# Sliding-window attention with a gated mixture: another order of the steps, one TensorE tiling, masks on other engines

## The chip, the cores and the metric

The kernel runs on one core of one Trainium2 chip. The metric is the device time of one execution in microseconds (us), the median of several runs. A core has five engines that run their own instruction queues side by side: TensorE (PE in the profile, with its weight loads as PEld), VectorE (DVE), ScalarE (ACT), GpSimd (POOL) and SyncE (SP, which here only issues transfers). An instruction that waits holds up everything behind it in its own engine's queue.

## The reference

```python
x = A_x                                    # [1, 2048, 512], bfloat16
g = sigmoid((x * gate_w).sum(-1))          # one gate per token
# A: attention, 32 heads of 16, query i sees keys i-255 .. i
qkv = x @ wqkv
scores = q @ k.T * 16 ** -0.5;  scores = where(mask, scores, -1e9)
a = softmax(scores) @ v @ wo
# B: the 8 tokens with the largest r = x @ w_r get a feed-forward, the others stay
y = (silu(x_sel @ w_gate) * (x_sel @ w_up)) @ w_down * sigmoid(r_sel)
b = x.at[idx].add(y)
out = g * a + (1 - g) * b                  # [1, 2048, 512]
```

## The kernel before

**Units of work.** The 512 channels are four chunks `c` of 8 heads, the 2048 tokens four blocks of 512. A *step* `s` is one chunk and one key block `qb`: there are sixteen, in the order `c = s // 4, qb = s % 4`, all of one chunk first. For its 16 groups of 32 keys a step computes the scores against the up to 288 queries that may see them (L717). Four heads share one matmul: `Kst` holds the keys four times, each copy masked to one head's 16 channels (L596, four DVE instructions per step). A step's scores form one stream of 4608 columns (3456 in the last block), cut into *units* of 512 columns, 136 in all. A unit has two halves of 64 channel rows, in PSUM banks 0 and 1 or 2 and 3 by turns; ACT takes the exponential of both (L731, 1024 columns) into `P`, which has two buffers, one for even and one for odd steps.

**Masks.** Where a group's window begins and ends, DVE takes the minimum of `P` and a pattern of 0 and 3e38 (L752), for every two units, with 64 columns a place.

**PV.** `pv_step` (matmuls at L771) accumulates one query block in two PSUM banks: first the eight last groups of the key block before (from the other `P` buffer), then the sixteen of its own. `Vbd` holds V by heads with columns of ones, so that the sums of the exponentials come out as extra rows. Then DVE copies the two banks to `OXY` (L801), four transfers collect the sums in `Dc`, DVE takes the reciprocal (L813), two transfers spread it over partitions as `Rb` (L814, L815), two more move the second half of `OXY`, and POOL multiplies into `OT` (L816). Steps 14 and 15 do the same by PE transposes in `norm_t` (L824 to L849).

**The rest.** `pair` runs two products side by side with 64x128 tiles of PE: keys and queries of a block (L582, copied out at L592 and L587), V (L606, copied at L613 and sent through memory to `Vbd`), and the output tiles (L663). The last four output tiles are `out_single` (L650, L656). `z_item` computes gate and router, `ffn` the feed-forward of the selected tokens, whose result is scattered into a copy of x in memory; `resid` loads that copy into `xr`, scales it by 1 - g (L633), and `out_evac` adds it to the gated output (L637) and stores it. A flag (L1021 to L1028) says whether all sums were in range; a general path (not taken) follows it.

**What sets the order.** Every operation is added to `Sched` with the tiles it reads and writes, an estimated duration and a priority. `schedule` lays them out in estimated time and so fixes each engine's queue; the chip then follows those queues, with semaphores. On PE the rule `pick_pe` takes score units first; other work goes by `prio` and a due unit `dl`, and PV is collected into bursts (`burst`), because a change of tiling is charged with `SWITCH = 106.0` ns. Banks 4 to 7 are handed out one by one (`acq`, `rel`); PV takes two and a `pair` takes two. `work` lists when each projection is due, in units: `U0(c, tc)` is the first unit of a step.

Of the kernel before, what the change touches and what calls it, by code (L numbers as in the profile page):

```python
# [49 lines left out]
class Sched:  # L50
# [6 lines left out]
    def __init__(self, nc, es, n_dma=40, banks=(4, 5, 6, 7), burst=2000):  # L57
        self.nc = nc
        self.ops = []
        self.last_w = {}  # L60
        self.readers = {}
        self.tick_sem = {e: es.enter_context(nc.semaphore("fk_" + e)) for e in self.ENGS}
        self.dsem = [es.enter_context(nc.semaphore("fd_%d" % i)) for i in range(n_dma)]
        self.nhw = n_dma
        self.dsem += [es.enter_context(nc.semaphore("fw_%d" % i)) for i in range(4)]
        self.free_banks = {b: [] for b in banks}
        self.burst = burst
        self.hold = 0.0
# [35 lines left out]
    def schedule(self):  # L104
# [13 lines left out]
        act_end = [0.0]  # L118
# [20 lines left out]
        def bank_ready(op):  # L139
            if not op.acq:  # L140
                return 0.0
            if len(self.free_banks) < len(op.acq):
                return None
            ts = sorted(max([u.t1 + self.SEM if u.done else 1e12 for u in us] or [0.0]) for us in self.free_banks.values())
            if ts[len(op.acq) - 1] >= 1e12:
                return None
            return ts[len(op.acq) - 1]
# [11 lines left out]
        def pick_pe():  # L159
            t = tfree["pe"]  # L160
            c = []
            hold = self.hold and any(o.kind == "V" and o.acq and o is vq[min(vp[0], len(vq) - 1)] and rdy(o) <= t + self.hold for o in cand["pe"])
            for o in cand["pe"]:
                if hold and o.acq and o.kind != "V" and o.prio >= 50:
                    continue
                b = bank_ready(o)
                if b is None:
                    continue
                c.append((max(rdy(o), b), o))
            if not c:  # L170
                return None
            S = [(s, o) for s, o in c if o.kind == "S"]
            V = [(s, o) for s, o in c if o.kind == "V"]
            F = [(s, o) for s, o in c if o.kind not in ("S", "V")]
            starve = act_end[0]
            s_ready = S and S[0][0] <= t + 30.0
            v = min(V, key=lambda z: z[1].id) if V else None
            if v is not None and v[0] > t + 40.0:
                v = None
            back = self.backlog(t)  # L180
            if v is not None and self.pe_mode == "V":
                room = starve - t
                if not s_ready and S == [] or room > 226 + 106 + 180 + v[1].dur:
                    return v[1], t
            if s_ready:
                return S[0][1], max(t, S[0][0])
            f = [(o.prio, o.id, o) for s, o in F if s <= t + 30.0]
            un = self.unow[0]
            urg = [z for z in f if z[2].dl is not None and un >= z[2].dl]
            if urg and self.pe_mode != "V":  # L190
                return min(urg, key=lambda z: z[:2])[2], t
            if v is not None and back >= self.burst:
                return v[1], t
            if f:
                return min(f, key=lambda z: z[:2])[2], t
            if v is not None and (back >= self.burst * 0.6 or not S):
                return v[1], t
            allc = [(s, o) for s, o in c if o.kind != "V"] or c
            s, o = min(allc, key=lambda z: (z[0], z[1].id))
            if v is not None and s > t + 400:  # L200
                return v[1], t
            if o.kind != "V" and V:
                sv, ov = min(V, key=lambda z: z[0])
                if sv + 300 < s and ov is min(V, key=lambda z: z[1].id)[1]:
                    return ov, max(t, sv)
            return o, max(t, s)

        self.unow = [0]
        vq = [o for o in ops if o.kind == "V"]
        vp = [0]  # L210

        def backlog(t):
            n = 0
            for o in vq[vp[0]:vp[0] + 60]:
                if o.done:
                    continue
                if o.acq and n:
                    break
                ok = True
                for d, sem in o.deps.items():  # L220
                    if d.kind == "V":
                        continue
                    if not d.done or (d.t1 + d.lat + (100.0 if d.dma else self.SEM)) > t + 40:
                        ok = False
                        break
                if not ok:
                    break
                n += o.cols
            return n
        self.backlog = backlog  # L230

        left = len(ops)
        while left:
# [10 lines left out]
            if e == "pe":  # L244
                if op.acq:
                    fb = sorted(self.free_banks, key=lambda b: (max([u.t1 if u.done else 1e12 for u in self.free_banks[b]] or [0.0]), b))
                    for bk in op.acq:
                        b = fb.pop(0)
                        us = self.free_banks.pop(b)
                        bk.i = b  # L250
                        for u in us:
                            op.deps[u] = True
                            start = max(start, u.t1 + self.SEM)
# [11 lines left out]
            for bk in op.rel:  # L265
                self.free_banks[bk.i] = [u for u in bk.users if u.eng != "pe"]
                dirty.add("pe")
            if not left or op.name is None and op.dur == 430:
                dirty.add("pe")
            if op.kind == "S":  # L270
                self.unow[0] += 1
            if e == "act" and op.kind == "E":
                act_end[0] = op.t1
                dirty.add("pe")
            while vp[0] < len(vq) and vq[vp[0]].done:
                vp[0] += 1
            for s in op.succ:
# [4 lines left out]
                if s.kind == "V":  # L282
                    dirty.add("pe")
# [99 lines left out]
NKB = 16  # L383
PADW = 32
STREAM = 16 * 288
PLEN = STREAM + 2 * PADW
# [4 lines left out]
def fast_path(nc, sem_es, flag, A_x, A_wqkv, A_wo, B_x, B_w_r, B_w_gate, B_w_up, B_w_down, gate_w, out):  # L391
# [4 lines left out]
    rs = nc.dram_tensor("fs_r", [16, 4096], F32, kind="Internal").ap()  # L396

    with ExitStack() as es:
# [9 lines left out]
        QT = sb("QT", [128, 2, 2048])  # L408
        Kr = sb("Kr", [128, 2, 512])
# [4 lines left out]
        Vbd = sb("Vbd", [128, 2, 64, 144])  # L414
        P = sb("P", [128, 2, 2, PLEN])
# [7 lines left out]
        kf = sb("kf", [128, 1], F32)  # L423
        xi = sb("xi", [128, 32], F32)
        NOX = 3
        OXY = sb("OXY", [128, NOX, 2, 512], F32)
        Dc = sb("Dc", [128, 2, 32], F32)
# [5 lines left out]
        xr = sb("xr", [128, 2, 4, 512])  # L433
        zb = xr[:, 0, 0, :]
# [18 lines left out]
        xsel = sb("xsel", [64, 512])  # L453
        xselT = sb("xselT", [128, 4, 32])
        WF1 = sb("WF1", [128, 4 * 1792])
        EG = sb("EG", [128, 1024], F32)
# [4 lines left out]
        ok1 = EG[:, 0:512]  # L461
        HT = xr[:, 1, 0, :].rearrange("p (b t) -> p b t", b=4)
        yq = zbf[0:8, :]
        WG = WF1[:].rearrange("p (k f) -> p k f", k=4)
# [8 lines left out]
        S.add("dve", lambda e: e.memset(zb, 0.0), w=[("xr", 0)], dur=150, prio=0)  # L473
# [12 lines left out]
        S.add("dve", lambda e: e.tensor_copy(out=kf[:], in_=hmi[:, 1:2]), r=["hmi2"], w=["kf"], prio=2)  # L486
        for i, (o_, w_) in enumerate(((ALU.is_lt, "MKb"), (ALU.is_ge, "MKa"))):
            S.add("dve", lambda e, i=i, o_=o_: e.tensor_scalar(out=MK[:, 32 * i:32 * i + 32], in0=xi[:], scalar1=kf[:, 0:1], scalar2=3.0e38, op0=o_, op1=ALU.mult),
                  r=["xi", "kf"], w=[w_], prio=2)
        MKR = ["MKa", "MKb"]  # L490
        for g in range(2):
            S.add("pool", lambda e, g=g: e.memset(P[:, g, :, 0:PADW], 0.0), w=[("padl", g)], prio=4)
            S.add("pool", lambda e, g=g: e.memset(P[:, g, :, PADW + STREAM:], 0.0), w=[("padr", g)], prio=4)

# [8 lines left out]
        S.add("pool", lambda e: e.memset(xsel[:], 0.0), w=["xsel"], dur=500, prio=20)  # L503
# [34 lines left out]
        for b in list(range(8)) + [4, 5, 6, 7, 4, 5]:  # L538
            S.add("pe", lambda e, b=b: e.matmul(ps[:, b, :], zb[:, 0:128], zb, start=True, stop=True), r=[("xr", 0)], w=[("warm", b)] + ([("S", b // 2)] if b < 4 else []), dur=430, prio=0,  # L539
                  mode="A", kind="F")  # L540
        for b in range(4, 8):
            S.free_banks[b].append(S.last_w[("warm", b)])


        def pair(A, B, prio, natom=4, dur=222.0, after=(), chain=None, gate=None, dl=None):

            bA, bB = Bank(), Bank()
            last = None
            for ph in range(2):
                for k in range(natom):  # L550
                    lo, hi = ((A, bA), (B, bB)) if ph == 0 else ((B, bB), (A, bA))
# [1372 lines left out]
```

## Time and profile before

| | |
|---|---|
| time, median of 3 runs | 198.92 us (197.67 to 199.78) |
| the profiled execution | 199.66 us, its span 196.9 us |
| granted PE clock, mean | 0.965 of full speed |
| busy, of the span | PE 164.1 us, DVE 142.8, ACT 127.3, POOL 26.8 |
| first exponential of the scores begins | 15.05 us after the span's start |
| last exponential ends | 162.6 us |
| last output addition ends | 190.6 us |

The span runs from the first to the last instruction of the program; the execution's time has some microseconds more. Busy time of PE counts overlapping matmuls once, from the first start to the last modelled end, so a PE that is 90% busy may still be fed with gaps. The times of single instructions in the profile are from this one execution.

### The profile page before, as it was taken

What the parts mean: (1) busy time and instruction counts of PE and PEld (TensorE: products, weight loads), DVE (VectorE), ACT (ScalarE), POOL (GpSimd) and SP (SyncE); (2) the same over time, 40 slices, a digit from 0 to 9 for tenths busy, and PEclk for the clock granted to TensorE, in tenths of its full rate; (3) what the DMA queues carried; (4) which work ended last, traced back from release to release, by engine and by line L of the source; (5) the groups of instructions that cost most, each with busy time, mean ns of one, the idle gap of its engine ahead of it and who ended that gap; (6) DMA issues with size and microseconds to landing.
All of it is one profiled execution on the core that took longest, in us unless ns stands there. A gap on an engine that the chain in (4) does not pass through costs nothing. (4 is left out here: it accounts for less than half of the span.)

```text
span 196.9 us, 6699 instructions
## 1 busy us (share of the span) xinstructions
PE 164.1 (83%) x2889; PEld 82.5 (42%) x2890; DVE 142.8 (72%) x365; ACT 127.3 (65%) x142; POOL 26.8 (14%) x42
## 2 busy tenths in 40 slices
PE   7889999997897998997992999778879973999910
PEld 2435555443353544553541545435345441534300
DVE  7569998997699949857534699687596454698870
ACT  3009999998599999283197598986999990000000
POOL 8400000010200202002212020032020204110000
PEclk9999999999999999999999699999999998799975
DMA  7998899993963943694678977742211232215840
GB/s 145 251 230 184 213 234 229 284 291 83 326 258 90 366 124 87 181 236 135 213 175 165 271 162 224 161 72 74 63 29 27 77 83 72 70 53 169 261 157 12
DMA packets 53058, 32.17 MB, mean 163 GB/s; under 512 B 37736, under 2 KB 49276, under 8 KB 52992
## 3 DMA queue, kind: packets, MB, share of 16 engines
q1 hardware_dynamic: 51376, 31.16, 60.1%
q10 hardware_dynamic: 1584, 0.52, 1.3%
q8 instruction: 23, 0.38, 0.9%
q14 instruction: 11, 0.09, 0.2%
q0 software_dynamic: 64, 0.02, 0.0%
HBM read 20.20 MB, written 9.42 MB: 150 GB/s over the span
## 5 line engine op out<-in xcount | busy, mean ns | idle before, releaser
L731 ACT ACTIVATE f_P<-f_ps 128x1024 bf16<-128x1024 f32 (+1 forms) x136 | 125.3, 1081 | 33.1 <-PE f_ps L771 16.7
L717 PE MATMUL f_ps<-f_QT,f_Kst 64*128 64x288 bf16 (+5 forms) x744 | 53.4, 244 | 9.6 <-ACT f_P L731 8.9
L752 DVE TENSOR_TENSOR f_P<-f_P,f_MK 128x512 bf16<-128x512 bf16 (+4 forms) x102 | 34.4, 355 | 24.4 <-ACT f_P L731 23.7
L771 PE MATMUL f_ps<-f_P,f_Vbd 64*34 64x288 bf16 (+8 forms) x1408 | 46.9, 251 | 4.6 <-DVE f_OXY L801 3.0
L717 PEld LDWEIGHTS f_ps<-f_QT,f_Kst 64*128 64x128 bf16 x744 | 21.4, 94 | 40.9 <-ACT f_P L731 33.3
L582 PE MATMUL f_ps<-f_XT,f_W 64*128 64x512 bf16 x256 | 37.0, 376 | 1.2 <-DVE f_QT L587 0.9
L771 PEld LDWEIGHTS f_ps<-f_P,f_Vbd 64*34 64x34 bf16 x1408 | 25.7, 94 | 26.2 <-issue 17.7
L816 POOL TENSOR_TENSOR f_OT<-f_OXY,f_Rb 128x512 bf16<-128x512 f32 x14 | 18.1, 1299 | 105.3 <-DMA f_Rb<-fs_r 105.3
L606 PE MATMUL f_ps<-f_W,f_XT 64*128 64x256 bf16 x256 | 17.8, 269 | 1.4 <-DMA f_XT<-in_A_x_dram 0.7
L596 DVE TENSOR_SCALAR f_Kst<-f_Kr,f_hm 128x512 bf16<-128x512 bf16 x64 | 18.6, 345 | 0.0
L801 DVE COPY f_OXY<-f_ps 128x512 f32<-128x512 f32 x28 | 18.2, 675 | 0.0
L663 PE MATMUL f_ps<-f_wo,f_OT 64*128 64x512 bf16 x96 | 13.5, 399 | 3.2 <-POOL f_OT L816 3.0
L582 PEld LDWEIGHTS f_ps<-f_XT,f_W 64*128 64x128 bf16 x256 | 10.9, 94 | 7.5 <-PE f_ps L582 1.9
L613 DVE CAST f_Vn<-f_ps 128x512 bf16<-128x512 f32 x16 | 10.5, 685 | 4.7 <-PE f_ps L606 4.7
L606 PEld LDWEIGHTS f_ps<-f_W,f_XT 64*128 64x128 bf16 x256 | 11.5, 94 | 5.5 <-DVE f_QT L587 1.4
L592 DVE CAST f_Kr<-f_ps 128x512 bf16<-128x512 f32 x16 | 10.7, 671 | 3.6 <-PE f_ps L582 3.6
L1032 ACT COPY f_sg<-f_ones_f 1x1 f32<-1x1 f32 x1 | 0.2, 190 | 17.5 <-DVE flag L1028 17.5
L813 DVE RECIPROCAL f_RC<-f_Dc 128x32 f32<-128x32 f32 x14 | 4.8, 345 | 9.2 <-DMA f_Dc<-f_OXY 9.2
L637 DVE SCALAR_TENSOR_TENSOR f_outt<-f_ps,f_g_f,f_xr 128x512 bf16<-128x512 f32 x16 | 11.3, 745 | 0.2
L587 DVE CAST f_QT<-f_ps 128x512 bf16<-128x512 f32 x16 | 10.9, 680 | 0.0
L663 PEld LDWEIGHTS f_ps<-f_wo,f_OT 64*128 64x128 bf16 x96 | 4.2, 97 | 9.0 <-POOL f_OT L816 3.1
L539 PE MATMUL f_ps<-f_xr 128*128 128x512 bf16 x14 | 5.5, 564 | 1.2 <-DVE f_hmi L476 1.2
(87 smaller groups left out, 76.2 us busy)
## 6 DMA issues: line engine op xcount, KB each, us to landing
fs_v<-f_Vn SPq DMA_DIRECT2D x8, 608.0 KB
f_Vbd<-fs_v SPq DMA_DIRECT2D x32, 144.0 KB, 3.2
f_Rb<-fs_r SPq DMA_DIRECT2D x14, 256.0 KB
f_xr<-fs_xc SPq DMA_DIRECT2D x4, 512.0 KB, 4.3
out_dram<-f_outt SPq DMA_DIRECT2D x16, 128.0 KB, 1.7
f_WF<-in_B_w_gate_dram SPq DMA_DIRECT2D x1, 1792.0 KB
f_OXY<-f_OXY SPq DMA_DIRECT2D x28, 64.0 KB, 4.3
f_WF<-in_B_w_up_dram SPq DMA_DIRECT2D x1, 1792.0 KB
```

What stands on the lines that cost most here:

```text
L582: return e.matmul(ps[:, bk.i, :], W[R, k, f0:f0 + 128], XT[R, k, 512 * tc:512 * tc + 512], start=first, stop=last, tile_position=(64 * h, ...
L587: S.add("dve", lambda e: e.tensor_copy(out=QT[:, c % 2, 512 * tc:512 * tc + 512], in_=ps[:, bk.i, :]), r=[("bk", id(bk))], w=[("QT", c % 2 ...
L596: S.add(eng, lambda e, j=j: e.tensor_scalar(out=Kst[:, s, :, j, :], in0=Kr[:, n % 2, :].rearrange("p (a k) -> p a k", k=32), scalar1=hm[:, ...
L606: return e.matmul(ps[:, bk.i, 256 * i:256 * i + 256], XT[R, kc, 128 * a:128 * a + 128], W[R, kc, 1024 + 256 * cp:1024 + 256 * cp + 256], s ...
L637: S.add("dve", lambda e: e.scalar_tensor_tensor(out=outt[:, a % 4, :], in0=ps[:, bk.i, :], scalar=g_f[:, a:a + 1], in1=xr[:, (a // 4) % 2, ...
L663: return e.matmul(ps[:, bk.i, :], OT[R, k, 128 * a:128 * a + 128], wo[R, k, :], start=first, stop=last, tile_position=(64 * h, 0), skip_gr ...
L717: ins = e.matmul(ps[:, sbk + v, so:so + m], Kst[R, ks, t, :, :].rearrange("p j k -> p (j k)"), QT[R, c % 2, q0:q0 + m], start=True, stop=T ...
L731: S.add("act", lambda e, p0=p0, n=n, sbk=sbk: e.activation(out=P[:, g, :, p0:p0 + n], in_=ps[:, sbk:sbk + 2, 0:n], func=ACT.Exp, scale=0.2 ...
L752: S.add("dve", lambda e, v=v, m=m: e.tensor_tensor(out=v, in0=v, in1=m, op=ALU.min), r=rd, w=[("M", g, r_[3]) for r_ in b], dur=60 + 2 * k ...
L771: ins = e.matmul(ps[64 * v:64 * v + 34, bk.i, q0:q0 + n], Vbd[R, cp, kh, 36 * q:36 * q + 34], P[R, g, v, PADW + o:PADW + o + n], start=fir ...
L801: S.add("dve", lambda e, b=b, bk=bk: e.tensor_copy(out=OXY[:, x, b, :], in_=ps[:, bk.i, :]), r=[("O", id(bX))], w=[("OXY", x, b, p) for p ...
L816: S.add("pool", lambda e: e.tensor_tensor(out=OT[:, c, 512 * qb:512 * qb + 512], in0=OXY[:, x, 0, :], in1=Rb[:, y, :], op=ALU.mult), r=[(" ...
```

## The change

**Order of steps.** A step is now `c = 2 * (s // 8) + s % 2, qb = s % 8 // 2`: chunks 0 and 1 block by block, then chunks 2 and 3. All queries stay in one tile `QK`; `P` has three buffers (a step reads the one before the last), `Vbd` four blocks, `OXY` four buffers. **PE.** Scores, projections, V and output all use 64x64 tiles, as PV does, so each of their matmuls becomes two; the rule for bursts goes, and PV is work with a due unit like the rest. PSUM banks 4 to 7 are handed out as two pairs, and one DVE instruction copies a pair. **Masks.** In steps 0 to 13 POOL multiplies `P` by 0 or 1 after the exponential; in steps 14 and 15 PE adds -3e38 to the scores. **Sums.** Two steps share one reciprocal; in most steps the sums go through memory (`ds`). **Space.** The feed-forward's weights and intermediate tiles lie in `xr` and `outt`; `xr` holds all four blocks.

```diff
-    def __init__(self, nc, es, n_dma=40, banks=(4, 5, 6, 7), burst=2000):
+    def __init__(self, nc, es, n_dma=40, banks=(2, 3)):
...
+            now = [z for z in c if z[0] <= t + 25.0]
+            if not now:
+                m = min(z[0] for z in c)
+                now = [z for z in c if z[0] <= m + 25.0]
+            s, o = min(now, key=lambda z: (z[1].kind != "S", z[1].dl if z[1].dl is not None else z[1].prio, z[1].id))
+            return o, s
...
+        NP = 3
+        P = sb("P", [128, NP, 2, STREAM])
...
+        WF1 = xr[:].rearrange("p q i f -> p (q i f)")[:, 0:4 * 1792]
+        EG = outt[:].rearrange("p a f -> p (a f)").bitcast(F32)
...
-                return e.matmul(ps[:, bk.i, :], W[R, k, f0:f0 + 128], XT[R, k, 512 * tc:512 * tc + 512], start=first, stop=last,
-                                tile_position=(64 * h, 0), skip_group_check=True)
+                return e.matmul(ps[64 * u:64 * u + 64, b, :], W[R, k, f0 + 64 * u:f0 + 64 * u + 64], XT[R, k, 512 * tc:512 * tc + 512], start=first, stop=last,
+                                tile_position=(64 * h, 64 * u), skip_group_check=True)
...
+        def cq(s):
+            return 2 * (s // 8) + s % 2, s % 8 // 2
+        U0 = [68 * (s // 8) + 9 * (s % 8) - (2 if s % 8 == 7 else 0) for s in range(NS)]
         TS = (14, 15)
+        DIRECT = (4, 5, 6)
+        POOLM = range(14)
...
+                    for x, (so, mc, m) in enumerate(mks):
+                        for v in range(2):
+                            R = slice(64 * v, 64 * v + 64)
+                            for w in range(2):
+                                C = slice(64 * w, 64 * w + 64)
+                                ins = e.matmul(ps[C, sbk + v, so:so + m], IDm[R, :], MB[R, mc:mc + m],
+                                               start=False, stop=(x == len(mks) - 1), tile_position=(64 * v, 64 * w), skip_group_check=True)
...
-                        S.add("dve", lambda e, v=v, m=m: e.tensor_tensor(out=v, in0=v, in1=m, op=ALU.min), r=rd, w=[("M", g, r_[3]) for r_ in b],
-                              dur=60 + 2 * k * w_ * 0.67, prio=1)
+                        S.add("pool", lambda e, v=v, m=m: e.tensor_tensor(out=v, in0=v, in1=m, op=ALU.mult), r=[("P", g, x) for x in us] + ["MK0", "MK1"],
+                              w=[("M", g) + x for r_ in bt for x in r_[3]], dur=130 + 2 * k * w_ * 2.3, prio=1)
...
+            op.dl = U0[s] + (LV if s < 8 else LW) + (tl[t][0] // 512 if s == s_src else 0)
...
-            for b, bk in enumerate((bX, bY)):
-                S.add("dve", lambda e, b=b, bk=bk: e.tensor_copy(out=OXY[:, x, b, :], in_=ps[:, bk.i, :]), r=[("O", id(bX))],
-                      w=[("OXY", x, b, p) for p in ("d", "o", "m")], dur=690, prio=4, use=(bk,), rel=(bk,))
+            S.add("dve", lambda e: e.tensor_copy(out=OXY[:, x], in_=ps[:, bk.i:bk.i + 2, :]), r=[("O", id(bk))],
+                  w=[("OXY", x, 0), ("OXY", x, 1), ("OXYm", x, 0), ("OXYm", x, 1)], dur=1220, prio=4, use=(bk,), rel=(bk,))
...
+            S.add("dve", lambda e: e.reciprocal(out=RC[:, s0:s + 1, :], in_=Dc[:, y]), r=Dk, w=[("RC", s0), ("RC", s)], dur=640, prio=3)
...
+        kq[0:2] = [(4, (0, 0, 1), (1, 1, 0)), (8, (0, 1, 0), (0, 1, 1))]
+        for dl, a, b in kq:
+            work.append((dl, 0, "kq", a, b))
         for cp in range(2):
             for tc in range(4):
-                work.append((U0(2 * cp, tc) - 8 if (cp, tc) != (0, 0) else -1, 1, "v", cp, tc))
+                work.append((U0[sidx(2 * cp, tc)] - VD if (cp, tc) != (0, 0) else 1, 1, "v", cp, tc))
         work.append((20, 2, "z"))
-        work.append((75, 2, "f"))
+        work.append((60, 2, "f"))
```

In a pair `(which, c, tc)` of `kq`, `which` is 1 for keys and 0 for queries: the second pair projects query block 1 of chunk 0 with the keys of chunk 1's first block.

## The prediction

> **What bounds it now.** I read the page's forty slices first, then the table by stage, then the waits, and last the timeline where an engine is dense.
>
> ```profile
> PE   7889999997897998997992999778879973999910
> ACT  3009999998599999283197598986999990000000
> POOL 8400000010200202002212020032020204110000
> L731 ACT ACTIVATE f_P<-f_ps 128x1024 bf16<-128x1024 f32 (+1 forms) x136 | 125.3, 1081 | 33.1 <-PE f_ps L771 16.7
> ACT f_P L731 <- PE f_ps L771: 16.7, 5, 7.2
> 80.00:90.00 10.00, 9.87 (x198) 5.28 (x194) 5.62 (x18) 5.73 (x7) 0.82 (x1) 1.00 0.81 204
> 170.00:180.00 10.00, 9.48 (x74) 3.79 (x73) 9.67 (x39) 0.00 (x0) 1.26 (x1) 1.00 0.23 70
> ```
>
> (The last two lines are the table by stage: window, length, then busy time of PE, PE's weight loads, DVE, ACT, POOL, then granted clock, DMA share, GB/s.) There are three stages. **Start:** the first exponential begins at 15.05. **Exponentials:** to 162.63, that is 147.6 us, of which ACT computes 126.4 (125.3 plus 1.1 for three small activations) and stands idle 21.2. The idle time is PE's: 16.7 us of it waits for the PV matmuls of L771, because an exponential may not overwrite a half of P that PV still reads, and in the 80 to 90 window PE is busy 9.87 of 10 while ACT has 5.73. **Tail:** from 162.6 to the last output addition at 190.6 (28.0 us) ACT does nothing and DVE is the dense engine (9.67 of 10): two steps of `norm_t`, sixteen output additions, the flag. Then 6.3 us to the end of the span for the last stores and the flag's readback. The profiled execution took 199.66 us for a span of 196.9, so 2.8 lie outside; the median shown is 198.92, 0.7 lower.
>
> **Part 1, one PE tiling.** The timeline shows what a change of tiling costs:
>
> ```profile
> 86.23 0.39 PE L717 MATMUL f_ps<-f_QT,f_Kst 64*128 64x64 bf16 x6
> 86.47 0.59 PE L582 MATMUL f_ps<-f_XT,f_W 64*128 64x512 bf16 x4
> ...
> 149.16 0.39 PE L717 MATMUL f_ps<-f_QT,f_Kst 64*128 64x128 bf16 x6
> 149.48 0.67 PE L771 MATMUL f_ps<-f_P,f_Vbd 64*34 64x288 bf16 x16
> 150.08 0.40 PE L717 MATMUL f_ps<-f_QT,f_Kst 64*128 64x192 bf16 x6
> ...
> 158.65 0.58 PE L771 MATMUL f_ps<-f_P,f_Vbd 64*34 64x32 bf16 x28
> ```
>
> A score unit is followed by a projection matmul (same 64x128 tiling) after 0.24 us, by PV (64x64) after 0.32; sixteen PV matmuls, four groups of at most 288 columns, should stream in 0.48 and take 0.60 until the scores start. So 0.09 to 0.1 us per change, and I count 158 changes between L771 and the other large matmuls: 15 us of PE time, removed. Against it the score, projection and output instructions double (744 to 1488, 512 to 1024, 96 at most to 192). Four 64x64 matmuls of a group already run together in PV: the last fenced line issues 28 matmuls, seven groups of 32 to 224 columns, in 0.58 us, of which the last alone is 0.26 long; 27 starts in 0.32 us is 12 ns each, close to the 0.28 that the columns need. I take nothing for the doubling; the other bound, the 38 ns per instruction at which L717 issues six in 0.23, would make each short group 150 ns and PE no better than before (rival B). Masks of the last two steps on PE: about 40 groups at some 0.03 each, 1.2 us, beside the exponentials.
>
> The Trainium skill speaks against this part: "TensorE: Matmul & The Clock Gate", section "Wait — 56ns, not 53.3ns?", says a matmul's start never follows another by less than about 25 ns. By it a group of four needs 100 ns, the 228 score groups under 240 columns lose 11 us, and the forecast would be 187; the 12 ns of the trace decide against it.
>
> PE's sum of large matmuls: scores 69,120 columns at 2.4 per ns is 28.8 (the 0.23 units above say 30), PV the same 30, sixteen projection pairs of 8 quads at 0.233 (32 matmuls in 3.88, less the last one's 0.38, over 15) 30, V eight pairs of 16 at 0.11 14, outputs 11, router and feed-forward 7: 122 us, some 112 of it between first and last exponential, beside ACT's 126. PE stops being the limit of that stage. Of the 21.2 idle us I keep 9.6, between 2 (only the wait for the P buffer that remains, since PV of step s must still free it before step s+1's second half) and 21 (as now).
>
> **Part 2, the order at the start.** Step 1 is now chunk 1. Query block 1 of chunk 0 is projected together with chunk 1's keys, whose weights SP issues at 12.56 and which take 5.4 to land (that row's median): 18.0. The pair's 8 x 0.233 with two score units between, 2.4, the copy of two banks 1.2, the scores 0.3: the sixth exponential, the first that reads query block 1, can start at 22.0; without a stall it would at 15.05 + 5 x 0.92 = 19.6. Price 2.4 us, between 0 (the weights come earlier in SP's queue) and 4.
>
> **Part 3, masks from DVE to POOL.** DVE loses 34.4 us (L752, 102 instructions) and, by merging two 0.675 copies into one of 1024 columns (bounds 1.03, without any fixed part, and 1.35; L917 with 448 columns takes 0.62, L866 with 512 0.69, so 1.02 ns a column and 0.16 fixed: 1.2), another 4: 143 becomes 104. POOL gets 27,648 elements per partition (2 halves x 1024 for twelve steps, x 768 for two). No POOL multiplication of this shape is in the trace. Low bound: the memset, 2432 elements in 2.12, 0.87 ns; high: affine_select, 128 in 0.41, 3.2 ns. Nearest is L816, also two inputs: 512 in 1.27, 2.3 ns plus some 0.13. That gives 64 + 108 x 0.13 = 78 us, with 18 of L816, 96 of the 113 that fourteen steps of exponentials take; per step 5.6 + 1.3 against ACT's 8.3. It hides under ACT, but PV, and behind PV in PE's queue the next scores, now wait for POOL. And POOL and DVE block each other:
>
> ```profile
> 1.58 4.18 POOL L498 MEMSET f_Vn<- 128x2432 bf16 x2
> 2.02 4.98 DVE L488 TENSOR_SCALAR f_MK<-f_xi,f_kf 128x32 bf16<-128x32 f32 x2
> ...
> 143.62 1.27 POOL L816 TENSOR_TENSOR f_OT<-f_OXY,f_Rb 128x512 bf16<-128x512 f32 x1 [6.85 <-DMA f_Rb<-fs_r]
> 143.63 1.54 DVE L752 TENSOR_TENSOR f_P<-f_P,f_MK 128x512 bf16<-128x512 bf16 x1 [0.21 <-ACT f_P L731]
> ```
>
> A mask of 0.42 took 1.54 because it began with L816 under way; a small tensor_scalar stood until 7.0, through the whole row of memsets. DVE keeps four tensor_scalar per step for Kst (1.13 us); if every such group pushes POOL by its length, POOL needs 8.0 of 8.3 us per step. I put 2 to 3 us of the 9.6 down to this; with the cover gone it is rival C.
>
> The Trainium skill agrees on the mechanism and sharpens it: "SBUF — State Buffer", Summary, says that whichever of the two starts first holds the shared port for its whole instruction. Sixteen Kst groups each meeting a 1.2 us mask would by that be an estimated 19 us of DVE, which has 104 of 150 to do; the sum does not change.
>
> **Part 4, order of the steps and the tail.** All four chunks of query blocks 0 and 1 are finished after steps 9 and 11, so their eight output tiles (PE 7.5, DVE 6) leave the tail for the exponential stage. Step 13 ends 14 units, 13 us, before the last exponential; in the trace the way from a finished copy (161.0) through sums, reciprocal and Rb to L816's end (173.3) is 12.2, so block 2 of OT comes some 4 us after the last exponential. DVE after it: one copy 1.2, `norm_t` 4 x 0.77 (reciprocal 0.20, two products 0.36, copy 0.21), singles 4 x 0.75, flag 1.8, block 2 4 x 0.72: 12.0, plus 2 of waits for the first transposes: 14, against 28. Low 11 (block 2 and the flag early), high 20 (both late and PE at half clock, as the granted 0.79 at the end shows now). SP issues 10 to 13 transfers per two steps instead of 16, and four loads of xr, which now need the feed-forward done first since its weights lie in xr; it ended near 100 and steps 8 to 11 still lie behind it.
>
> **Sum.** 15.0 + 126.4 + 2.4 + 9.6 + 14 + 6.3 = 173.7 of span, + 2.8 = 176.5; against the median rather than this execution 176.
>
> **Rivals.** *B, the exponential stage stays as long*, because PV waits for POOL where PE waited for itself, or the doubled instructions cost what the changes did: idle 21 again beside the 2.4 of the start, 187. For it: only two PSUM pairs for everything, one held by PV most of a step. Against: PE has 14 us to spare. *D, the tail stays*: block 2 of OT comes 12 us late behind slower DMA (two hops for the sums in some steps, and the trace has DVE waiting 4.4 us for Dc at L813); 24 instead of 14, 186. *C, slower: POOL becomes the bound.* Place: the masks of steps 0 to 13. From 17 us on POOL works without pause, and after its last mask come a copy, 12.2 of normalization, two output pairs and the end, 25 us. Then the time is 17 + 27,648 p + 32 + 25 + 2.8, which passes 198.9 at p = 4.4 ns an element; at 5 ns it is 215. For it: rows of 64 elements, port waits. Against: no POOL row of 128 or more elements is above 3.2. *That the change does nothing*, for instance because the old order was not PE's doing, has little room: the tail's work moves whatever PE does.
>
> **Chances.** Forecast 0.60, its own range 167 to 185; B 0.20; D 0.08; C 0.12. Range 167 to 193: it takes in B and D and leaves out C's far part and a stall-free 165. A measurement of this kernel tells about 1% from no change; faster by more 0.85, within 0.03, slower 0.12.
>
> **What would show it.** Right: PE rows of 64*64, no 0.1 us gaps between L771's successors and the scores, ACT idle after its first instruction near 12 us, POOL busy near 105 with masks of 0.13 us plus 2.3 ns an element, DVE near 105, output additions from about 115 us on, 14 us between last exponential and last addition. Wrong: masks above 3.2 ns, PE idle behind POOL, ACT idle above 20, or a tail above 20.

## The result, and the profile after

The kernel after took 207.13 us (median; 204.32 to 209.57) beside 199.05 for the kernel before: a ratio of 1.029, interval 1.022 to 1.037. This ratio and those below are formed from the fast, undisturbed executions alone (204.9 us in the middle for the kernel after), and where fewer than two of a kernel are left, none is given. Forecast were 176. On the chip of the first experiments the same kernel took 200.73 beside 199.53 (1.007, 0.999 to 1.015). So the loss is small or nothing there, and the ratio of one kernel differs by 2% between two chips; the forecast is missed by 31 us on the one and 25 on the other. The profiled execution of after took 209.33 us, more than the median; sizes are therefore taken from the first experiment, the control (the same kernel, run again), whose profiled execution took 200.33.

The forty slices and rows of after's page (rows: busy us, mean ns; then idle us before them and who ended it):

```profile
PE   7986998899967887499836889869858679679960
ACT  2044399899967999299925899888848873000000
POOL 8312065846635489349713488596565004130000
PEclk9996999699999999799979999999988966955997
L710 ACT ACTIVATE f_P<-f_ps 128x1024 bf16<-128x1024 f32 (+1 forms) x136 | 127.3, 1037 | 41.4 <-PE f_ps L691 37.8
L726 POOL TENSOR_TENSOR f_P<-f_P,f_MK 128x64 bf16<-128x64 bf16 (+3 forms) x106 | 72.5, 699 | 64.5 <-ACT f_P L710 64.3
L539 DVE TENSOR_SCALAR f_Kst<-f_QK,f_hm 128x512 bf16<-128x512 bf16 x64 | 27.2, 486 | 0.2
```

ACT's idle time is now ended by scores (L691), 37.8 of 41.4 us; PV, which ended 16.7 us before, ends 1.2. TensorE has holes in slices 17 and 21 (4 and 3 tenths), where ACT falls to 2 and 2. Terms of the forecast against the two profiles of the same kernel, in us:

| | forecast | after | control |
|---|---|---|---|
| first exponential begins | 15.0 | 13.0 | 12.9 |
| first to last exponential | 138.4 | 160.0 | 152.5 |
| last exponential to last output addition | 14 | 27.8 | 26.4 |
| to the end of the span | 6.3 | 6.4 | 6.5 |
| outside the span | 2.8 | 2.1 | 2.0 |

Two terms failed: the exponential stage by 14 to 22 us and the tail by 12 to 14.

**Where TensorE stops.** The timeline of the control, at two of the holes (start, length, engine, line, matmul; in brackets the idle time before it and what ended it):

```profile
78.62 0.29 PE L743 MATMUL f_ps<-f_P,f_Vbd 64*34 64x128 bf16 x9
81.25 0.21 PE L743 MATMUL f_ps<-f_P,f_Vbd 64*34 64x64 bf16 x3 [2.34 <-issue]
...
98.07 0.41 PE L691 MATMUL f_ps<-f_QK,f_Kst 64*64 64x128 bf16 x11
101.28 0.20 PE L691 MATMUL f_ps<-f_QK,f_Kst 64*64 64x96 bf16 x1 [2.79 <-issue]
```

A unit of twelve score matmuls stops after the eleventh and goes on 2.8 us later, with no semaphore in between ("issue"). The waits put 16.3 us on stops without a semaphore in the control, 19.4 in after, 0.2 in the kernel before. The page's row of a DMA queue that carries instructions (packets, MB, share), before and then after; its count of packets goes with the number of TensorE's instructions in every run:

```profile
q8 instruction: 23, 0.38, 0.9%
```

```profile
q8 instruction: 35, 0.57, 1.3%
```

Each packet is 16 KB. Matmuls and weight loads together are 5779 before and 8739 in the control; over the packets that is about 250 each. Counting these instructions up to each pause (over 0.9 us from one start to the next, between 18 and 168 us) shows what the pauses have in common:

```
control: begin (us), length (us), place within 256 instructions
 37.12 1.27 .69 |  54.20 1.64 .68 |  78.71 2.53 .65 |  98.28 3.00 .64
106.30 2.01 .62 | 109.89 0.92 .11 | 132.03 1.34 .61 | 136.37 1.01 .61
143.86 2.28 .60 | 150.78 0.94 .61 | 156.81 1.43 .59 | 162.01 1.32 .59
after:  8 of 9 pauses at .59 to .68, 18.7 us     before: 0 of 5
```

Eleven of twelve lie at the same place of a 256-instruction period, whatever matmul runs there; a wait for another engine has no reason to. The trace's records of the instruction queue fit. A packet mostly starts between .84 of a period and .5 of the next. Ten of the eleven pauses end 1.3 to 1.7 us after a packet has landed, and all eight of after 1.2 to 1.6; where the packet starts only when TensorE is already dry (78.75 and 98.50, at .65 and .64; landed at 79.78 and 99.78) the pause is longest. And in none of the seventeen profiles of this case does a packet start while more than some 285 instructions are left before the next such place: TensorE has about one block ahead of it when the next is fetched. When it uses that block up faster than the next one arrives, it runs dry.

The Trainium skill, "Runtime: NRT & Kernel Launch", section "Instruction fetch mechanics", has blocks of 16 KB and 256 instructions, room for 2048 instructions (eight blocks) on TensorE, and calls the crossing of a block mostly hidden. The size of the blocks agrees with the packets here. For the rest the measurement decides: about one block ahead, not eight, and 18.8 us of pauses at the crossings.

After a long pause the granted clock is lower too: in the control 3.4 us at half clock begin 0.8 to 1.3 us after the end of each of the three longest pauses. Two windows of after, one in the stage behind such a pause and one in the tail, where no pause of that length stands before it (window, length, busy us of PE, its loads, DVE, ACT, POOL; clock, DMA share, GB/s):

```profile
80.00:90.00 10.00, 6.69 (x184) 4.43 (x176) 4.77 (x9) 5.39 (x7) 4.46 (x11) 0.83 0.62 216
...
180.00:190.00 10.00, 8.29 (x58) 3.74 (x61) 8.14 (x35) 0.00 (x0) 2.53 (x2) 0.56 0.19 65
```

**The tail.** The first output matmul and the first output addition of after, with the last exponential ending at 173.04:

```profile
172.39 1.95 PE L608 MATMUL f_ps<-f_wo,f_OT 64*64 64x512 bf16 x16
...
175.60 0.75 DVE L581 SCALAR_TENSOR_TENSOR f_outt<-f_ps,f_g_f,f_xr 128x512 bf16<-128x512 f32 x1 [9.63 <-PE f_ps L608]
```

No output tile had left the tail, where the forecast had eight of sixteen "from about 115 us".

### The profile page after: what moved, and what is told of

Its sections match the earlier page's. It is cut to its first block, busy times and chain, and to the rows that moved or that the text cites. A ratio compares the mean times of both kernels' runs of the same rounds, so it can differ in the third digit from the quotient of the medians.

```text
span 207.2 us, 9562 instructions
## 1 busy us (share of the span) xinstructions
PE 164.5 (79%) x4370; PEld 106.8 (52%) x4370; DVE 121.5 (59%) x222; ACT 129.5 (62%) x142; POOL 98.2 (47%) x144
## 4 chain that ended last, share of the span: by engine, by line
PE 48%; ACT 24%; issue 11%; DVE 7%; SPq 5%; DMA 2%
ACT f_P L710 24%; PE f_ps L743 12%; PE f_ps L691 11%; PE f_ps L519 9%; PE f_ps L608 6%; SPq L442 5%; PE f_ps L550 4%; DMA f_wrg<-in_B_w_r_dram 2%; PE f_ps L935 1%; DVE f_outt L581 1%; PE f_ps L594 1%; DVE f_QK L533 1%; DVE f_OXY L807 1%; PE f_ps L844 1%; DVE f_Kst L539 1%
## 5 line engine op out<-in xcount | busy, mean ns | idle before, releaser
L710 ACT ACTIVATE f_P<-f_ps 128x1024 bf16<-128x1024 f32 (+1 forms) x136 | 127.3, 1037 | 41.4 <-PE f_ps L691 37.8
L726 POOL TENSOR_TENSOR f_P<-f_P,f_MK 128x64 bf16<-128x64 bf16 (+3 forms) x106 | 72.5, 699 | 64.5 <-ACT f_P L710 64.3
L691 PE MATMUL f_ps<-f_QK,f_Kst 64*64 64x288 bf16 (+4 forms) x1488 | 59.4, 254 | 16.3 <-issue 8.1
L691 PEld LDWEIGHTS f_ps<-f_QK,f_Kst 64*64 64x64 bf16 x1488 | 33.9, 111 | 33.4 <-ACT f_P L710 19.8
L519 PE MATMUL f_ps<-f_XT,f_W 64*64 64x512 bf16 x512 | 39.4, 401 | 0.5 <-DVE f_zf L900 0.2
L533 DVE CAST f_QK<-f_ps 128x1024 bf16<-128x1024 f32 x16 | 19.5, 1221 | 27.0 <-PE f_ps L519 27.0
L539 DVE TENSOR_SCALAR f_Kst<-f_QK,f_hm 128x512 bf16<-128x512 bf16 x64 | 27.2, 486 | 0.2
L773 DVE COPY f_OXY<-f_ps 128x1024 f32<-128x1024 f32 x14 | 17.0, 1212 | 16.8 <-PE f_ps L743 13.8
L550 PE MATMUL f_ps<-f_W,f_XT 64*64 64x256 bf16 x512 | 20.0, 271 | 2.9 <-issue 2.6
L519 PEld LDWEIGHTS f_ps<-f_XT,f_W 64*64 64x64 bf16 x512 | 14.5, 112 | 9.0 <-PE f_ps L519 1.6
L608 PE MATMUL f_ps<-f_wo,f_OT 64*64 64x512 bf16 x192 | 15.8, 463 | 0.1
```

The lines of the kernel that those rows point to most:

```text
L519: return e.matmul(ps[64 * u:64 * u + 64, b, :], W[R, k, f0 + 64 * u:f0 + 64 * u + 64], XT[R, k, 512 * tc:512 * tc + 512], start=first, sto ...
L533: S.add("dve", lambda e: e.tensor_copy(out=bass.AP(QK, 512 * slot(ia), [[18 * 512, 128], [512 * (slot(ib) - slot(ia)), 2], [1, 512]]), in_ ...
L539: S.add("dve", lambda e, j=j, n=n: e.tensor_scalar(out=Kst[:, n % NKS, :, j, :], in0=QK[:, 16 + n % 2, :].rearrange("p (a k) -> p a k", k=32),
L550: return e.matmul(ps[64 * u:64 * u + 64, bank, 256 * i:256 * i + 256], XT[R, kc, q:q + 64], W[R, kc, 1024 + 256 * cp:1024 + 256 * cp + 256 ...
L608: return e.matmul(ps[64 * u:64 * u + 64, bank, :], OT[R, k, q:q + 64], wo[R, k, :], start=first, stop=last, tile_position=(64 * h, 64 * u) ...
L691: ins = e.matmul(ps[C, sbk + v, so:so + m], Kst[R, ks, t, 2 * w:2 * w + 2, :].rearrange("p j k -> p (j k)"), QK[R].rearrange("p a f -> p ( ...
```

## The experiments

Theory F: the doubled instructions arrive too late. Rivals: POOL's masks hold TensorE up; the pauses follow the bytes on the DMA queues, not the count. A ratio is to the kernel before on the same chip, with its 95% interval. "That place" is .57 to .70 of a 256-instruction period. The experiments ran on four chips, the control on one of them; differences of 2% between experiments of different chips are therefore not read as effects.

**1. Control** (after, unchanged).

> The kernel after, unchanged, as the measure for the others on this chip. Theory F (fetch): TensorE's instructions come by DMA in blocks of 16 KB, and the doubled count makes TensorE run dry: 205 to 207 us, 35 blocks, exponential stage near 160 us, pauses of TensorE in the middle of matmul groups that add up to 15 to 20 us, each ending 1 to 2 us after a block has landed. Rival P (POOL): TensorE waits for late masks, by their length or by the port; then the pauses stand at PV matmuls behind a mask, and not beside blocks.

The ratio is 1.007 (0.999 to 1.015); 200.7 us and a stage of 152.5 are less than expected. The pauses are those listed above: eleven at that place, 18.8 us in sum. They stand at scores (6.5 us) as much as at PV (6.3), which rival P does not expect, and ten of them end behind a packet, as theory F does.

**2. Large loads left out.**

```
-  dma_start(WU, B_w_up ...)              # 1.8 MB
+  dma_start(WU[0:8], B_w_up[0:32] ...)
-  dma_start(WDv, wdv[:, 0:14, :])        # 1.6 MB
+  dma_start(WDv[0:8], wdv[0:8, 0:14, :])
```

> The kernel after, with the loads of the feed-forward's up and down weights cut to 8 partitions (5 per cent of the bytes; the feed-forward's values are left out in effect). All instructions and their order stay. Theory F says that the two longest pauses (3.5 and 4.1 us, at 82 and 103 us) are long because the block queues behind these loads: they fall to 1 to 2 us or go, and the time by 4 to 7 us, to 199 to 203; the pauses without a large load beside them stay. If the DMA load has nothing to do with the pauses: within 1.5 us of the kernel after.

0.963 (0.956 to 0.969), 191.8 us: more than expected. Both pauses, at 79 and 98 us, are gone (the one at 106 comes at 100 now and is 1.5), the sum at that place goes from 18.8 to 10.9, and the exponential stage from 152.5 to 145.1: 7.9 us of pause, 7.4 of stage. If the remaining 10.9 went at the same rate the stage would be some 134 to 135 (an estimate), below the 138.4 of the forecast.

**3. The same loads in pieces**, all values computed, four pieces a few score units apart; and once more with the output pairs due earlier (`dl=60 + a` for `dl=150 + a`).

```
+  for k_ in range(4):
+      lgates.append((S.dma(... WU[:, k_, :] ...), (54, 58, 62, 66)[k_]))
```

> The kernel after, with each of the three feed-forward weight loads cut into four pieces, and the pieces of the up and down weights held back to score units 54, 58, 62, 66 and 72, 75, 78, 81 (about 4 us apart). All values are computed. The kernel's own planner sees no difference (its plan ends 0.1 us later). Theory F: the block of instructions queues behind 0.45 MB and not 1.8 MB, so the pauses at 79 and 98 us (2.5 and 3.0 us in the control) fall to 1.5 us or less, and the time by 2 to 5 us, to 196 to 199; less than the 9 us of the run without these loads, since the bytes still move. If only the bytes count, wherever they lie: 200 to 202.

> The kernel after with the feed-forward's weights in pieces (as in the earlier run of that edit, 195.2 us) and the output pairs due at unit 60+a; the start as it is. The pieces give 2 to 3 per cent against the kernel before, the outputs another 0 to 2 us (3 of 16 additions moved ahead of the last exponential in the run that had them): 192 to 197. If the pauses fall anew by chance with every small change of the queue, as in the run that moved the start: anywhere from 192 to 203, in one run and another.

0.986 (0.967 to 1.005), median 195.2, and 0.987 (0.981 to 0.993), median 198.2, the second above its expectation. The pauses fall to 14.8 and 14.5 us. Pieces seem to help by some 2%, which the intervals hardly separate from the control; the longest pause of the first is now 3.1 us at 56, eight us after the copy of x was issued.

**4. Masks cut to two columns** of 64 or 32 (values left out, instructions and waits kept).

```
-  v = AP(P, ..., [288, k], [1, w_]])
+  v = AP(P, ..., [288, k], [1, 2]])
```

> The kernel after, with the masks on GpSimd cut from 64 or 32 columns to 2 (same instructions, waits and order; the masks are left out in effect). Rival P: late masks or the shared port hold TensorE up; then the time falls by 8 us or more, to below 193. Theory F: masks are beside the point, since each pause of over 1 us ends after a block of instructions: GpSimd's busy time falls by some 55 us, the Kst copies on VectorE go from 486 back to 345 ns, and the time falls by no more than 3 us, to 197.5 to 201.

Rows of the Kst copies and of POOL's masks:

```profile
L539 DVE TENSOR_SCALAR f_Kst<-f_QK,f_hm 128x512 bf16<-128x512 bf16 x64 | 19.0, 360 | 0.2
L726 POOL TENSOR_TENSOR f_P<-f_P,f_MK 128x4 bf16<-128x4 bf16 (+2 forms) x106 | 23.5, 232 | 107.9 <-ACT f_P L710 107.2 <-ACT f_sg L863 0.6
```

The time is 198.9 to 203.4 us, where rival P asked for less than 193: no gain. POOL lost 49 us of work, the copies got faster (503 ns in the control to 360), and the pauses are all there: 20.6 us in ten, at .59 to .68. POOL's lateness falls as a cause of the pauses; so does rival C of the prediction.

**5. Scores alone back in 64x128**, in the kernel after.

```
-  for w in range(2): matmul(ps[C, ...], Kst[R, ks, t, 2*w:2*w+2, :], ..., tile_position=(64*v, 64*w))
+  matmul(ps[:, ...], Kst[R, ks, t, :, :], ..., tile_position=(64*v, 0))
```

> The kernel after with the scores back in two 64x128 matmuls, all else as it is. Matmuls 4370 to 3626, blocks of instructions 35 to 29, and some 150 changes of tiling come back, at 0.1 us each where they are not covered. Theory F: pauses inside matmul groups fall from 16 us to 8 to 12 us, the changes cost 5 to 10: 197 to 205, TensorE's busy time about as it was. If the count of instructions does not matter: pauses stay at 16 us or more and the time goes to 206 to 215.

```profile
q8 instruction: 29, 0.48, 1.0%
```

1.002 (0.996 to 1.007). There are 29 packets and two pauses at that place with 4.0 us in sum. 15 us less of pauses shorten the stage by only 3.3 us, to 149.2: the changes of tiling are back, 228 of them where some 150 were expected, and no time is gained.

**6. Projections, V and output as 128x128**, scores and PV as they are.

> The kernel after, with projections, V and output projection as single 128x128 matmuls (one where four of 64x64 stood, two to four of them together), scores and PV as they are. Matmuls fall from 4370 to some 3100, blocks from 35 to some 26, at the price of tiling changes (about 120 groups by up to 0.2 us, 10 to 24 us of TensorE, of which half may lie beside exponentials). Theory F: pauses in the middle of groups below 5 us in sum, 190 to 202 us. Rival P: pauses stay, changes come on top, 207 to 215.

1.003 (0.994 to 1.013), 28 packets. 12.7 us of stops without a semaphore are left, more than expected, four of them 2.2 to 2.6 us long at .53 to .59. With one packet fewer than in 5 there is more standing still, so it is not the count over the whole run that decides; the scores and PV, where the short matmuls are, still have the density of the kernel after.

**7. The tiling undone as a whole**, the order of steps and queue of after kept.

```
-  for u in range(2): x[0][0](e, ..., h, u, ...)     # 64x64, and the scores as in 5
+  x[0][0](e, ..., h, ...)                           # 64x128
```

> The kernel after with Part 1 undone as a whole: scores, projections, V and output projection in two matmuls of 64x128, PV in 64x64, the order of steps and the order of TensorE's queue as in the kernel after. Matmuls fall from 4370 to some 2890, blocks of instructions from 35 to 23. Theory F: pauses inside matmul groups below 3 us (16 in the control), changes of tiling back with 10 to 15 us of TensorE in their place: 193 to 203, within 3 per cent of the kernel after; that would say that the tiling as a whole gave nothing. If the tiling was worth what Part 1 says (15 us) the time goes to 208 to 216.

0.962 (0.953 to 0.970), 192.0 us: less than expected. Three pauses stand at that place, 3.4 us. ACT waits 2.3 us for PV:

```profile
ACT f_P L706 <- PE f_ps L739: 2.3, 2, 2.0
```

From PV to the next scores TensorE's starts are now 210 ns apart in the mean (59 cases) against 123 in the control (70), from scores to PV 160 (46) against 60 (61): the change of tiling costs the 0.09 to 0.1 us that Part 1 said. There are 105 such neighbours, and 152 changes of tiling of all kinds in the stage (14 us at 0.09 to 0.1 each), and yet the stage, 147.2 us, is 5 us shorter than the control's, in a profiled execution of 197.9 us, 6 above the median.

**8. The same with a planner that knows the two tilings** (0.106 us for a change, among equals the tiling that is loaded) and output pairs due at 60+a.

```
-  min(now, key=(kind != "S", dl, id))
+  min(now, key=(kind != "S", dl > un + 2, mode != self.pe_mode, dl, id))
```

> As the last, but the kernel's planner is told of the two tilings (0.106 us for a change, and among equals the tiling that is loaded), and the output pairs are due at unit 60+a. The planner's own end is 0.5 us after that of the kernel after, with all changes counted in, so only what it does not know comes on top; without pauses that should be 10 to 15 us against 25 now: 186 to 194, below the kernel before. If the changes cost more than 0.106 us: 195 to 203.

0.948 (0.939 to 0.958), 190.2 us median, with nothing left out: better than both kernels. Its tail is 20.8 us, with four additions ahead of the last exponential.

**9. The kernel before with the 64x64 tiling alone.**

> The kernel before with one change only: scores, projections, V and output projection in four 64x64 matmuls where two of 64x128 stood. Nothing else moves. The prediction's Part 1 says 184 to 191 us (8 to 15 us of tiling changes gone, nothing for the doubling). Theory F: blocks of instructions rise from 23 to some 31, pauses in the middle of matmul groups of 5 to 15 us appear that the kernel before does not have, and the gain is eaten: 194 to 206 us. Rival P has no POOL masks here and expects what the prediction says, 184 to 191.

1.027 (1.017 to 1.037): slower, where Part 1 had 8 to 15 us of gain. Its waits:

```profile
ACT f_P L736 <- PE f_ps L776: 15.9, 6, 6.4
...
PE f_ps L902 <- DMA f_xsel<-in_A_x_dram,f_idxT: 4.5, 1, 4.5
```

TensorE did get about 10 us back between lines (intervals under 0.5 us at which one line follows another in the stage: 52 to 41 in sum), but ACT still waits 15.9 us for PV, 16.7 before: that wait was not set by the changes of tiling. 4.6 us of pauses at .58 to .67 came on top, slightly less than expected, and one wait of 4.5 for the feed-forward's gather, whose index left SyncE's queue 4.7 us later than in the kernel before; why is open, so this run does not weigh the pauses.

**10. The kernel before with its masks on POOL alone.**

> The kernel before with its masks on GpSimd (a product with 0 or 1 in place of a minimum), nothing else. VectorE's busy time falls by 30 us, GpSimd's rises to some 100 to 110. The prediction's Part 3 takes nothing for this while GpSimd stays hidden; the kernel before waits for PV matmuls in its exponential stage, and PV now waits for masks that take 2.3 ns an element instead of 0.6: 197 to 204. Rival P (POOL holds TensorE up): above 206.

```profile
L596 DVE TENSOR_SCALAR f_Kst<-f_Kr,f_hm 128x512 bf16<-128x512 bf16 x64 | 30.1, 528 | 0.0
...
L752 POOL TENSOR_TENSOR f_P<-f_P,f_MK 128x512 bf16<-128x512 bf16 (+4 forms) x102 | 80.4, 807 | 47.4 <-ACT f_P L731 46.4 <-ACT f_sg L880 0.7
```

1.029 (1.022 to 1.035), 204.4 us. VectorE's busy time falls by 14 us, not 30: 34.4 of masks go, and the Kst copies take 11.5 more (345 to 528 ns); the rest of the difference is open. Moving the masks is no gain by itself, but a loss of 3% in the old order.

**11. The start's loads earlier**, and with that the pieces, and then all large loads in pieces.

```
-  load_w(1, c, 1, "sp", 30 + c, after=5000 ...)     # chunk 1
+  load_w(1, 1, 1, "act", 3, after=0)
-  work.append((20, 2, "z"))
+  work.append((30, 2, "z"))
```

> The kernel after, with the query and key weights of chunk 1 loaded from the queue of ScalarE at the start instead of 5 us later from SyncE's, and the router's matmuls due at unit 30 instead of 20. Theory S (start): TensorE's queue stands at the router's matmuls, which wait for their weights, and at the projection that waits for chunk 1; the delay of 2.5 to 3.5 us that units 0 to 10 have against the plan falls to about 1 us, and the time by 2 to 3 us. If it is hidden by later pauses: within 1 us of the control's 200.7.

> The kernel after with three edits together: weight loads in pieces, the start's loads earlier, and output pairs due at unit 60+a instead of 150+a, so that TensorE takes them as soon as their inputs are there. Theory: pieces 2 to 5 us, start 2 to 3, output pairs 1 to 3 (the planner says 2.8 for start and outputs): 191 to 196. First output addition before the last exponential, by 3 to 6 us in the plan; if the blocks of OT are late by their chain of transfers, after it, and the third term is nothing.

> The kernel after with all of its large loads in pieces that are 3 to 5 score units apart (the feed-forward's three weights, and the copy of x in DRAM), the weights of chunk 1 third in SyncE's queue, the router due at unit 30 and the output pairs due at unit 60+a. All values are computed. Theory F: no pause above 2.5 us is left; against the run that split the feed-forward's weights alone (195.2 us) the pause at 56 us (3.1, beside the copy of x) falls to 1.5, the start gains 2 and the outputs 1 to 2: 189 to 194, below the kernel before. If the pauses only move to other places, as in the run that moved the start: 195 to 200.

207.4 us (202.4 to 209.5), 199.2 (196.0 to 202.0), 199.3 (192.6 to 203.2): all three miss what was expected. In the first the delay of units 0 to 10 does go, though the first exponential comes 1.1 later; and then pauses of 3.9 and 5.7 us stand at 42 and 54 us, both at .69, the second five us after the copy of x was issued. A likely reason is that a change of the queue shifts all later packets against the loads; no run shows it by itself. The executions of the last kernel alone spread from 192.6 to 203.2, so a gain of 2 or 3 us can't be read from runs of this kind.

**12. The reciprocal sums not waited for**, output pairs due at 60+a (the normalization is left out in effect).

```
-  in1=Rb[:, z, :]      # r: ("Rb", z)
+  in1=ones, broadcast
```

> The kernel after with GpSimd's multiplication for OT taking a constant 1 where it waited for the reciprocal sums to come back through DRAM (the normalization of steps 0 to 13 is left out in effect; the transfers still run), and the output pairs due at unit 60+a. Theory T (tail): the tail stays at 26 us because OT of blocks 0 and 1 is finished only 21 to 27 us after the last PV copy of its step, behind a chain of transfers, near or after the last exponential. With the chain gone OT of block 0 is there by 135 us, 6 to 8 of the 16 output additions lie before the last exponential, and the tail falls from 26.4 to 16 to 20 us, the time to 190 to 197. If TensorE or its two PSUM pairs hold the outputs up and not the chain: tail 22 to 26.

0.985 (0.978 to 0.992), median 198.3. Eight additions lie before the last exponential and the tail is 18.6 us, both as expected; but not all of that is the chain's. The granted clock in the tail was 1.00 here and 0.83 in the control. The first run of 3 had 1.00 too, and with no addition moved its tail is 22.0 us (control, then that run):

```profile
165.40:191.80 26.40, 23.23 (x259) 10.46 (x252) 20.56 (x58) 0.19 (x1) 5.07 (x5) 0.83 0.30 97
...
164.60:186.60 22.00, 19.60 (x260) 8.97 (x248) 19.10 (x57) 0.24 (x2) 2.63 (x3) 1.00 0.33 110
```

So of the 7.8 us some 4.4 go with the clock and 3.4 with the eight additions (an estimate from single executions). OT of block 0 was complete at 150.8, not 135. The wait that is left is for the OXY transfers, which SyncE issues 10.6 and 12.8 us after the end of the PV copy, behind some fifteen other transfers. With the due unit alone (the second of 3, then 8, and the last two of 11) three or four additions move and the tail is 20 to 23. So the due unit and the chain each hold outputs back; what each is worth in time is open.

## Why the prediction was wrong, point by point

**Part 1, the doubling: the step that failed.** "I take nothing for the doubling" looked only at how fast TensorE can start matmuls (12 ns), and that held: the doubled scores follow each other in 19.8 ns on average against 37.7, under the 25 ns that the prediction weighed, so a unit takes as long as before. Not looked at was where the instructions come from. In the kernel before 256 instructions last 5 to 10 us, in the control mostly 3 to 5, and TensorE runs dry eleven times. Cutting bytes (2, and less clearly 3) or instructions (5, 7) shortens the pauses at exactly that place in the count; cutting masks does not. Bytes alone do not make them: the kernel before moves 32.2 MB, the control 32.5, and only one has the pauses. So the exponential stage was 152.5 to 160.0 us where the sum had 138.4: ACT stands idle 25 us of it in the control, and the sum had 2.4 and 9.6.

**Part 1, the changes.** 0.1 us each is right, 15 us of TensorE about right, their worth not. In the order of before, taking them away left ACT's wait for PV as it was (9). In the new order they are spread over the units, and ACT's 0.92 us of work per unit can cover them in part, while a pause of 2 to 4 us outlasts the two score units, 1.8 us, that ACT has at most in store (two halves of PSUM); this reason is argued, not measured apart. Measured is that 15 us of pauses cost more than some 14 us of changes: 7 against 1 is 4.5% in favour of the old tiling (0.962 against 1.007, on two chips). What had made TensorE look like the limit (9.87 of 10 busy, 16.7 us of ACT waiting for PV) went with the rest of the change, most likely the order and the third P buffer, and not with the tiling: in 7, with both tilings in use, ACT waits 2.3 us for PV.

**Part 2.** Right in the control: the sixth exponential was to start at 22.0 and starts at 21.9 (24.4 in after). The first is 2 us earlier than assumed, so ACT stands idle 4.2 us between the two, not 2.4; 1.2 of these follow on TensorE's wait for the router's weights (0.97 us), which the forecast did not name.

**Part 3.** The mask's price is right within 8%: 2.3 ns an element plus some 0.13 us gave 78, measured 72.5 (the rows fit 1.9 ns and 0.2 us better: 64 columns 0.32, 512 columns 1.20); POOL 98 of some 105. VectorE is 121 to 125, not 104: the Kst copies, 486 to 503 ns instead of 345, take 9 to 10 of the difference, half of the 19 us estimated for the case that each meets a mask; the rest is open. Rival C had little room, and 4 shows that it has none.

**Part 4, the second step that failed.** The eight output tiles of blocks 0 and 1 did not leave the tail. Step 9's last exponential ends at 111.6 in the control. Its PV copy begins at 124.9 (PV is due up to 17 units late by design), and OT is complete 26.7 us after the copy's end, where the sum had 12.2 from a place where SyncE's queue was nearly empty:

```profile
138.66 1.29 SPq L793 DMA_DIRECT2D f_OXY<-f_OXY  x2
...
145.46 0.63 SPq L799 DMA_DIRECT2D f_Rb<-fs_r  x1
```

```profile
151.57 1.27 POOL L800 TENSOR_TENSOR f_OT<-f_OXY,f_Rb 128x512 bf16<-128x512 f32 x1
```

The OXY transfers are issued 12.6 us after the end of the copy. By the code they wait for the transfers of the sums (Dc) whose rows they overwrite, the last of which SyncE issues at 131.1; and they stand in its queue behind those of step 10, whose copy ends only at 134.5. How the 12.6 us divide between the two is open. Block 1 is complete at 167.9, after the last exponential. And block 0, ready 13 us before the last exponential, isn't taken: its pairs are due at unit 150+a (`a` is the number of the output tile), beyond the 136 units there are. That line stood in the code to be read.

Two more terms were mis-sized. The sum has one PV copy and one `norm_t` behind the last exponential; in the control those of steps 14 and 15 both come there (copies at 168.9 and 170.1), 4.3 us more, and VectorE is busy 20.6 us of the tail, not 12.0. And the clock granted in the tail, 0.83 in the control and 0.79 in after, stood in the high bound of 20 only; by 12 it is worth some 4 us.

**Rivals.** B named the right term ("the doubled instructions cost what the changes did") with another mechanism, D the tail at its old length; the forecast gave them 187 and 186 one at a time, and both came true together: 176.5 + 11 + 10 is 197, 3 us below the control. The range held one failure at a time and had no room for both.

## What to carry to other kernels

Price a change that multiplies instructions twice: by what the engine needs to start them, and by the rate at which they have to arrive; packets of the instruction queue over the span, against the length of the densest stretch of 256, say how near it is (here 256 instructions took 3 to 5 us in the control, with pauses, and 5 to 10 in the kernel before, without). A cost that is spread out in small pieces beside another engine's work can be cheaper than the same sum in a few long stops. A tile "finished after step n" leaves the tail only if its whole chain of transfers, in the queue's order and by its due time, is read too.

## What the hardware showed that was not expected

TensorE's instructions come in packets of 16 KB, about 256 instructions, each 0.9 to 1.8 us under way in the control, and about one such block ahead of their use. In the kernels with all products in 64x64 tiles and the new order, TensorE went dry .57 to .70 into a period in nearly every pause, whatever ran there, and went on, in most, 1.2 to 1.7 us after the packet had landed. Over all runs these pauses were 0.9 to 2.7 us where the packet had started before TensorE was dry, 2.5 to 5.7 where it started only then. That a large load delays the packet is shown by experiment 2 for two pauses; what the packet waits for in the queues is not.
